# Kernel study: sketched linear attention, Fourier mix and MLP on one core — another form of the MLP, another handing-out of PSUM banks, wider q features, and the order of steps made for them

## The chip, the cores and the metric

One Trainium2 chip, one core of it. Times are device microseconds (us) of one execution, and the profile's span is about 1.8 us shorter than the time of the same run. A run is called slow when its time is more than 1.5% above the fastest run of the same kernel. The medians quoted are of all runs, the ratios of fast ones.

PE is the tensor engine, PEld its weight loads, DVE the vector engine, ACT the scalar engine, POOL the GpSimd engine. Memory outside the core is reached by DMA.

## The reference, cut to what matters

```
# per batch (4), head (4), 1088 rows, head size 32, sketch size 8
a, b   = S1 @ x, S2 @ x                      # 8 values each, for x = q and for x = k
phi(x) = outer(a, b)                         # 64 features
kv, z  = sum over rows of phi(k) x v, of phi(k)
out    = (phi(q) @ kv) / (phi(q) @ z + 1e-6)
# all heads side by side: x is (4, 1088, 128)
u  = x + real(fft over 128 of fft over 1088 of x)
un = (u - mean(u)) / sqrt(var(u) + 1e-6)     # per row
y  = u + relu(un @ w_ch1) @ w_ch2            # 128 -> 512 -> 128
```

## The kernel before

The kernel is one list of small steps for four batches, in attention (features of k and q, `kv`, numerator and denominator), Fourier mix and MLP. Every step has a name, and the text `ORDER` says in which order they are put down. The traces looked at here show the engines taking their own instructions in that order, so the text decides which work stands in an engine's queue.

```
ORDER = """
wm1 wm1 wm1 wm1 wm1 wm1 wt wm1 (...) kT0.0 pkr0 pab0.0 kT0.1
(... 7 lines cut ...)
qp2.3 q2.4 qa2.4 qp2.4 kT3.0 kv2.0 bb0.0 st0.0 kpr1 rs0.0 un0.0 kv2.1 kv2.2 bb0.1 st0.1 kc2 kt2 kz2
rs0.1 un0.1 tr0.0 nd2.0 ut0.0 rc2.0 mh0.0.0 re0.0.0 re0.0.1 mh0.0.1 re0.0.3 re0.0.2 nd2.1 rc2.1
(... 13 lines cut ...)
"""
for name in ORDER.split():
    step[name]()
```

Step names: `wm` warm-up matmul, `wt` sketch weights, `kT`, `qT` transposes, `pab`, `ka`, `kp` features of k (matmul, copy, product), `q`, `qa`, `qp` features of q, `kv`, `kc`, `kt`, `kz` the sums, `nd`, `rc` numerator and division, `fo` folding, `a`, `z`, `zr` the transform over rows. The MLP has eight groups of four tiles and two rests: `bb` u, `st` statistics, `rs` root, `un` normalized u, `tr` its transposition, `ut` copy (`ud` on DVE), `mh` hidden matmuls, `re` or `rd` relu, `mm` output matmuls, `ot` output copy.

PSUM in three pools of two buffers each; w has buffers of two banks:

```python
ps_w = ctx.enter_context(tc.tile_pool(name="ps_w", bufs=2, space=PSUM))   # pq, ph, pz: two banks each
ps_g = ctx.enter_context(tc.tile_pool(name="ps_g", bufs=2, space=PSUM))   # pab, pkr, pkv, pt, pnd, put
ps_u = ctx.enter_context(tc.tile_pool(name="ps_u", bufs=2, space=PSUM))   # pu
```

The MLP (cut): the group's u is normalized, transposed on PE, goes through the hidden layer, and the output is added to u in PSUM.

```python
def st(self):
    for i in range(self.nt):
        nc.vector.bn_stats(stats[:, :], self.pu[:, i, :])
        nc.vector.bn_aggr(self.mv[:, i, :], stats[:, :])
def rs(self):    # rstd = sqrt(var + eps), on ACT
def norm(self):  # un
    nc.vector.reciprocal(rstd[:, 0:nt], rstd[:, 0:nt])
    for i in range(nt):
        nc.vector.tensor_scalar(out=self.un[:, i, :], in0=self.pu[:, i, :],
                                scalar1=self.mv[:, i, 0:1], scalar2=rstd[:, i : i + 1],
                                op0=SUB, op1=MULT)
def tr(self):
    for i in range(self.nt):
        nc.tensor.transpose(self.put[:, 128 * i : 128 * i + 128], self.un[:, i, :], ident_b[:, :])
def ut(self, copy=nc.scalar.copy):
    copy(self.unT[:, 0:n], self.put[:, 0:n])
def m1(self, c2):                       # two hidden chunks into two banks
    for c in range(2):
        nc.tensor.matmul(ph[:, c, 0:n], w1_b[:, ...], self.unT[:, 0:n], start=True, stop=True)
def m2(self):
    for i in range(self.nt):
        for cc in range(4):
            nc.tensor.matmul(self.pu[:, i, :], self.ht[:, cc, ...], w2_b[:, cc, :], start=False, stop=(cc == 3))
```

The q features are made in four steps of 256 columns and one of 2 x 32 for each batch.

## Time and profile before

| | before |
|---|---|
| time, median of 3 runs | 140.47 us (139.18 to 143.3) |
| span of the profiled run | 138.7 us, granted clock 0.973 |
| PE busy, of the whole span | 108.0 us, 78% |
| PE busy in the middle, 9.34 to 110.3 us | 85.40 of 100.96 us |
| PE idle in the middle | 15.6 us |

The page of the kernel before: the span, the busy time of each engine (share of the span, instructions), and PE's busy tenths in 40 equal slices of the span.

```profile
span 138.7 us, 3380 instructions
...
PE 108.0 (78%) x1324; PEld 73.8 (53%) x1333; DVE 84.7 (61%) x249; ACT 62.2 (45%) x149; POOL 41.0 (30%) x86
...
PE   6795898899769979967789999299798677767520
```

No engine is full. The row of tenths shows where: PE is mostly at 7 to 9 tenths through the middle and falls to 6 to 7 in the last quarter. For the argument, the span is cut in three: a start up to the first feature matmul (in after up to the end of the warm-ups, 0.2 us past it), a middle up to the last matmul of the row transform, and a tail of MLP groups only. This is the view by stretches: length, busy us (instructions) of PE, PEld, DVE, ACT, POOL, then granted clock, DMA share and GB/s.

```profile
core 0: us, PE busy (x) PEld busy (x) DVE busy (x) ACT busy (x) POOL busy (x), PEclk, DMA share, GB/s
0.00:9.34 9.34, 7.34 (x21) 2.69 (x21) 4.18 (x16) 1.28 (x1) 8.43 (x31) 1.00 0.72 162
9.34:110.30 100.96, 85.40 (x1167) 62.40 (x1172) 65.44 (x176) 46.56 (x114) 31.33 (x54) 0.98 0.31 66
110.30:138.70 28.40, 15.26 (x140) 8.73 (x141) 15.11 (x58) 14.32 (x34) 1.29 (x2) 0.93 0.15 43
```

PE is busy 85% of the middle. Its 15.6 idle us (100.96 − 85.40) are the largest sum of idle time in the kernel. The view of PE's waits in the middle, longest in total first (us in total, times, longest):

```profile
engine line waited for: us in total, times, longest us
PE put L514 <- DVE un L507: 2.3, 1, 2.3
PE pab L280 <- DVE kp L290: 1.6, 1, 1.6
PE pnd L428 <- DVE xf L451: 1.4, 2, 1.1
PE pkv L397 <- DVE kpr_244 L290: 1.1, 1, 1.1
PE pnd L428 <- DVE kp L290: 1.1, 2, 0.7
```

Kinds of wait are listed there, of 0.2 to 2.3 us. What one looks like is seen in the timeline (start, length, engine, line, operation, and in brackets the idle time before it and who ended it):

```profile
61.81 0.41 PE L514 MATMUL put<-ident_b,un 128*128 128x128 bf16 x4
...
62.20 0.21 ACT L420 COPY kvz_94<-pt 64x66 f32<-64x66 f32 x1
...
63.58 0.30 ACT L499 ACTIVATE rstd<-mv,bias_eps 128x4 f32<-128x4 f32 x1 [1.17 <-DVE mv L494]
63.90 0.58 ACT L520 COPY unT<-put 128x512 bf16<-128x512 bf16 x1
...
64.54 1.02 PE L529 MATMUL ph<-unT,w_b 128*128 128x512 bf16 x3 [0.92 <-ACT unT L520]
```

The transposition (`put`) is over at 62.22 us. The copy that the hidden matmuls wait for starts only at 63.90, because it stands in ACT's queue behind the root of the *next* group (`rstd`), for which ACT sat idle for 1.17 us. PE then waits 0.92 us. The copy itself takes only 0.58 us.

Two groups of instructions that the change touches (busy us, mean ns, idle us before):

```profile
L374 DVE TENSOR_TENSOR qpT<-pq,qa 128x512 f32<-128x512 f32 x16 | 11.0, 687 | 14.1 <-ACT qa L368 14.0
...
L368 ACT COPY qa<-pq 128x512 f32<-128x512 f32 x16 | 9.2, 585 | 9.0 <-PE pq L357 8.9
```

And two lines of the timeline at the start, the first transposes of k and the first feature matmuls:

```profile
7.88 1.30 DVE L337 STREAM_TRANSPOSE kT<-kin_80 128x512 f32<-128x512 f32 x2 [1.89 <-DMA kin_80<-in_k_dram]
...
9.34 1.05 PE L280 MATMUL pab<-sblk,kT 128*128 128x128 f32 x8
```

### The profile page before, as it was taken

How to read it: one execution, taken by the hardware profiler on the slowest of the kernel's cores; microseconds unless marked ns; L12 is line 12 of the kernel's file. 1: busy time of each engine (PE TensorE's matmuls, PEld its weight loads, DVE VectorE, ACT ScalarE, POOL GpSimd, SP SyncE). 2: the span in 40 equal slices, each digit the busy share in tenths (PEclk: the TensorE clock that was granted, in tenths of full speed). 3: DMA queues.
4: the chain of work that ended last, by engine and by line, in shares of the span. 5: the costliest groups of instructions: out<-in, count | busy, mean ns of one | idle time of the engine just before them, and what ended most of it. 6: DMA issues, size and time to landing. Idle time of an engine off the chain costs nothing.

```text
span 138.7 us, 3380 instructions
## 1 busy us (share of the span) xinstructions
PE 108.0 (78%) x1324; PEld 73.8 (53%) x1333; DVE 84.7 (61%) x249; ACT 62.2 (45%) x149; POOL 41.0 (30%) x86
## 2 busy tenths in 40 slices
PE   6795898899769979967789999299798677767520
PEld 2254567587557635845777467078654434434310
DVE  5238828978489473698695326837661684584720
ACT  2101236189745653634664460244433068738320
POOL 7998980000930010700564130002443030000000
PEclk9999999999999999999999999959999999999995
DMA  3989979989800000000011200000202000220221
GB/s 113 237 134 216 210 157 222 174 165 254 139 4 7 0 0 0 5 0 5 0 43 37 72 3 5 0 0 2 61 19 74 2 19 5 66 69 19 76 59 38
DMA packets 27968, 9.40 MB, mean 68 GB/s; under 512 B 20400, under 2 KB 26928, under 8 KB 27952
## 3 DMA queue, kind: packets, MB, share of 16 engines
q1 hardware_dynamic: 26912, 8.66, 27.5%
q0 software_dynamic: 672, 0.26, 1.6%
q10 hardware_dynamic: 368, 0.27, 0.8%
q8 instruction: 10, 0.16, 0.5%
q14 instruction: 6, 0.05, 0.2%
HBM read 7.22 MB, written 2.23 MB: 68 GB/s over the span
## 4 chain that ended last, share of the span: by engine, by line
PE 45%; DVE 28%; POOL 9%; ACT 9%; issue 4%; another core or an unknown queue 0%; POOLq 0%; ACTq 0%; DVEq 0%
PE pq L357 11%; PE pnd L428 7%; DVE un L507 6%; PE pu L544 5%; PE pkv L397 5%; PE pz L572 5%; DVE stats L493 5%; DVE kp L290 4%; PE ph L529 4%; DVE mv L494 4%; POOL kq L177 3%; PE pz L574 2%; ACT qa L368 2%; DVE qT L342 2%; ACT ht L534 2%
## 5 line engine op out<-in xcount | busy, mean ns | idle before, releaser
L374 DVE TENSOR_TENSOR qpT<-pq,qa 128x512 f32<-128x512 f32 x16 | 11.0, 687 | 14.1 <-ACT qa L368 14.0
L534 ACT ACTIVATE ht<-ph 128x512 bf16<-128x512 f32 (+1 forms) x30 | 14.8, 565 | 6.1 <-PE ph L529 3.9
L368 ACT COPY qa<-pq 128x512 f32<-128x512 f32 (+1 forms) x20 | 10.1, 521 | 9.2 <-PE pq L357 9.1
L493 DVE BATCH_NORM_STATS2 stats<-pu 128x6 f32<-128x128 f32 x34 | 9.4, 276 | 7.0 <-PE pu L597 3.3
L544 PE MATMUL pu<-w_b,ht 128*128 128x128 bf16 x136 | 10.7, 220 | 3.5 <-ACT ht L534 2.4
L357 PE MATMUL pq<-qT,wa 32*64 32x256 f32 (+1 forms) x192 | 12.2, 338 | 0.5 <-DVE qpT L374 0.4
L529 PE MATMUL ph<-unT,w_b 128*128 128x512 bf16 (+1 forms) x34 | 9.0, 350 | 4.0 <-ACT unT L520 3.1
L507 DVE TENSOR_SCALAR un<-pu,mv,rstd 128x128 bf16<-128x128 f32 x34 | 11.8, 406 | 0.4
L357 PE MATMUL pq<-qT,wb 32*64 32x256 f32 (+1 forms) x192 | 11.4, 322 | 0.0
L290 DVE TENSOR_TENSOR kp<-ka,pab 128x1024 f32<-128x1024 f32 x8 | 9.7, 1207 | 2.9 <-ACT ka L286 2.9
L544 PEld LDWEIGHTS <-ht 128*128 128x128 bf16 x136 | 8.0, 98 | 6.0 <-ACT ht L534 3.8
L280 PE MATMUL pab<-sblk,kT 128*128 128x128 f32 x64 | 9.0, 284 | 2.3 <-DVE kp L290 1.6
L499 ACT ACTIVATE rstd<-mv,bias_eps 128x4 f32<-128x4 f32 (+1 forms) x10 | 3.0, 297 | 17.1 <-DVE mv L494 17.1
L280 PEld LDWEIGHTS pab<-sblk,kT 128*128 128x128 f32 x64 | 7.8, 191 | 3.4 <-DVE kp L290 1.8
L514 PE MATMUL put<-ident_b,un 128*128 128x128 bf16 x34 | 5.9, 225 | 4.8 <-DVE un L507 3.6
L286 ACT COPY ka<-pab 128x128 f32<-128x128 f32 (+1 forms) x10 | 2.5, 254 | 13.6 <-PE pab L280 13.6
L191 PE MATMUL warm<-wdummy 128*128 128x512 bf16 x18 | 7.2, 577 | 1.2 <-DVE wdummy L144 1.2
L445 DVE TENSOR_SCALAR rc<-pnd 128x8 f32<-128x8 f32 (+1 forms) x20 | 3.2, 160 | 7.8 <-PE pnd L428 4.9
L539 DVE TENSOR_SCALAR ht<-ph 128x512 bf16<-128x512 f32 (+1 forms) x10 | 4.5, 482 | 5.7 <-PE ph L529 3.9
L514 PEld LDWEIGHTS <-un 128*128 128x128 bf16 x34 | 2.9, 96 | 8.5 <-DVE un L507 8.0
L357 PEld LDWEIGHTS pq<-qT,wb 32*64 32x64 f32 x192 | 6.2, 132 | 2.0
L451 DVE TENSOR_TENSOR xf<-pnd,rc 128x256 f32<-128x256 f32 x16 | 6.8, 424 | 0.7
(245 smaller groups left out, 232.8 us busy)
## 6 DMA issues: line engine op xcount, KB each, us to landing
out_dram<-ot SPq DMA_DIRECT2D x32, 64.0 KB, 2.0
qin_76<-in_q_dram SPq DMA_DIRECT2D x1, 544.0 KB, 5.6
qin_77<-in_q_dram SPq DMA_DIRECT2D x1, 544.0 KB, 5.1
qin_78<-in_q_dram SPq DMA_DIRECT2D x1, 544.0 KB, 6.6
qin_79<-in_q_dram SPq DMA_DIRECT2D x1, 544.0 KB, 4.7
vin_84<-in_v_dram SPq DMA_DIRECT2D x4, 128.0 KB, 3.4
kin_81<-in_k_dram SPq DMA_DIRECT2D x4, 128.0 KB, 3.3
vin_85<-in_v_dram SPq DMA_DIRECT2D x4, 128.0 KB, 5.3
```

The lines of the kernel that those rows point to most:

```text
L280: nc.tensor.matmul(_v(self.ps, 0, 128, 32 * j, [[256, 2], [128, 2], [1, 32]]), lhsT, sblk2, start=True, stop=True, skip_group_check=True)
L290: nc.vector.tensor_tensor(out=_v(self.out, 0, 128, 0, [[64, n], [8, 8], [1, 8]]), in0=_v(self.ka, 0, 128, 0, [[8, n], [1, 8], [0, 8]]), in ...
L357: nc.tensor.matmul(pq[f0 : f0 + 64, g % 2, w, n * i : n * i + n], wt[32 * g : 32 * g + 32, :, :], self.qT[32 * g : 32 * g + 32, pr, c0 : c ...
L368: nc.scalar.copy(self.qa[c][:, :, 0:m], self.pq[c][:, :, 0, 0:m])
L374: nc.vector.tensor_tensor(out=qpT[:, prs[0], :, c0 : c0 + n], in0=pq[:, :, 1, 0:n], in1=qa[:, :, 0:n], op=MULT)
L428: nc.tensor.matmul(pnd[:, 2 * a + pr, :], self.qpT[:, pr, a, 32 + 128 * c : 160 + 128 * c], kvz[:, pr, :], start=True, stop=True, skip_gro ...
L493: nc.vector.bn_stats(stats[:, :], self.pu[:, i, :])
L507: nc.vector.tensor_scalar(out=self.un[:, i, :], in0=self.pu[:, i, :], scalar1=self.mv[:, i, 0:1], scalar2=rstd[:, i : i + 1], op0=SUB, op1 ...
L514: nc.tensor.transpose(self.put[:, 128 * i : 128 * i + 128], self.un[:, i, :], ident_b[:, :])
L529: nc.tensor.matmul(ph[:, c, 0:n], w1_b[:, 128 * cc : 128 * cc + 128], self.unT[:, 0:n], start=True, stop=True)
L534: nc.scalar.activation(out=self.ht[:, cc, 0:n], in_=self.ph[cc // 2][:, cc % 2, 0:n], func=ACT.Relu)
L544: nc.tensor.matmul(self.pu[:, i, :], self.ht[:, cc, 128 * i : 128 * i + 128], w2_b[:, cc, :], start=False, stop=(cc == 3), skip_group_chec ...
```

## The change

Its intent: to take the normalization out of the chain in front of the hidden layer, to let any step use any free PSUM bank, and to halve the number of q steps.

1. MLP. u is built twice, once as before and once transposed, straight from the transform, so that nothing has to be normalized before the first matmul. The weight is centred beforehand (which takes the mean out), and 1/std, being positive, passes through the relu and is applied to the output, with the sum, on DVE.
2. One PSUM tile of eight banks; a free bank is picked when a step is put down, always the one that has been free longest.
3. q features in 512 columns: two steps and a rest for each batch.
4. At the start, k of batch 0 is issued ahead of S on ACT's queue.
5. The text `ORDER` is made anew, all 23 lines of it (26 after).

```diff
 ORDER = """
-wm1 wm1 wm1 wm1 wm1 wm1 wt wm1 wm1 wm1 wm1 wm1 wm1 wm1 wm1 wm1 wm1 wm1 wm1 kT0.0 pkr0 pab0.0 kT0.1
-ka0.0 kp0.0 pab0.1 qT0 ka0.1 kp0.1 q0.0 qa0.0 kT1.0 qp0.0 ktr0 kv0.0 pbr0 kar0 q0.1 qa0.1 q0.2 kv0.1
+wm1 wm1 wm1 wm1 wt wm1 wm1 wm1 wm1 wm1 wm1 wm1 wm1 wm1 wm1 kT0.1 wq qT0.1 qT0.0 kT0.0 pab0.1 w1 wm1
+pkr0 wm1 wm1 wm1 pab0.0 ka0.1 ka0.0 ktr0 tf0 kT1.0 kT1.1 kp0.1 tfd kp0.0 qT1.0 qA0.1 qA0.0 qB0.0
 (... all other lines replaced too; cut ...)
+class Banks:
+    def __init__(self, n):
+        self.clock, self.at = n, list(range(n))
+    def take(self, n):
+        starts = [i for i in range(0, len(self.at), n)
+                  if all(a is not None for a in self.at[i : i + n])]
+        b0 = min(starts, key=lambda i: max(self.at[i : i + n]))
+        for i in range(b0, b0 + n):
+            self.at[i] = None
+        return b0
+    def drop(self, bn):
+        self.clock += 1
+        for i in range(bn[0], bn[0] + bn[1]):
+            self.at[i] = self.clock
-    ps_w, ps_g, ps_u = (three pools, as above)
+    pall = psum.tile([128, 8, 512], FP32, name="pall")
+    banks = Banks(8)
 (... start ...)
-    nc.scalar.dma_start(s12[...], S1), (s12[...], S2)      # first on ACT's queue
+        # after the four loads of k of batch 0, two of which are on ACT's queue:
+        nc.scalar.dma_start(s12[...], S1), (s12[...], S2)
 (... q features ...)
-    self.qa[c] = sb2.tile([128, 2, 256], FP32, name="qa", tag="qa")
+    self.qa[pr] = sb2.tile([128, 2, 512], FP32, name="qa", tag="qa")
 (... MLP ...)
+        def us(self, copy=nc.scalar.copy):      # u to SBUF, its bank comes free
+            copy(self.u_s[:, 0 : self.nt, :], self.pu[:, 0 : self.nt, :])
+            banks.drop(self.bnu)
-                nc.vector.bn_stats(stats[:, :], self.pu[:, i, :])
-                nc.vector.bn_aggr(self.mv[:, i, :], stats[:, :])
+                nc.vector.bn_stats(stats[:, i, :], self.u_s[:, i, :])
+            (four small operations for all tiles of the group give DM * var)
-        def tr(self):    # PE transposes of un
+        def tt(self):    # u transposed, from z, eight matmuls
-            nc.tensor.matmul(self.pu[:, i, :], self.ht[...], w2_b[:, cc, :], start=False, ...)
+            nc.tensor.matmul(self.pm[:, i, :], self.ht[...], w2_b[:, cc, :], start=(cc == 0 and i == 0), ...)
-            copy(ot[:, 0:nt, :], self.pu[:, 0:nt, :])
+            nc.vector.scalar_tensor_tensor(out=ot[:, i, :], in0=self.pm[:, i, :],
+                                           scalar=rstd[:, i : i + 1], in1=self.u_s[:, i, :], op0=MULT, op1=ADD)
```

## The prediction

> **What bounds it now.** No engine is full: the page shows PE 108.0 us (78% of 138.7), DVE 84.7, ACT 62.2. By stretches, PE is 88% busy from 14.4 to 58.2 us, 87% to 86.9, 78% to 108.5, but 67% from 108.5 to 133.7. Front and middle are nearly bound by PE; the last 25 us are latency. There the chain of waits repeats, per group of four tiles: stats and aggregate 1.7 us, rstd 0.3, reciprocal 0.2, un 1.37, transpose 0.23, copy 0.59, ph 0.5, four relus 2.04, pu matmuls 1.0, ot 0.58: about 8.5 us, one group each 5 us.
>
> **What changes, with costs.**
> 1. MLP. u is also built transposed, straight from z, so statistics, root and reciprocal leave the chain before the first matmul; 1/std (positive, so it passes through the relu) is applied at the end. Estimated chain: 0.9 (transposed u) + 0.6 copy + 0.6 + 2.0 relus + 0.3 (last matmuls, now chunk by chunk behind the relus) + 1.5 (scale-and-add, like un: 4 at 0.34, plus a reciprocal) = 5.9, about 2.7 shorter. Work hardly falls: transposes (0.23 streamed) become eight wider matmuls (0.67, estimate): PE +3.5 us in all. ACT trades ot copies for copies of u to SBUF. DVE: un becomes the final add; the aggregates become four small operations of about 0.2. Fewer DVE relus, -2.7; more DVE copies, about +2.7.
> 2. q in 512 columns: qa is 585 ns at 512 elements and 265 at 128, so 1012 at 1024 (estimate): ACT -1.3 us; qpT 687 at 512, about 1207 at 1024 (as kp shows): DVE -1.3. PE streams as many columns in half the matmuls (24, not 48, a batch): perhaps -1 us.
> 3. Banks by age: three pools of two buffers become one pool of eight banks. The Trainium skill ("PSUM — Partial Sum Buffer", Terms) gives eight 2 KiB banks and one matmul output of at most one bank, so 512 f32 columns fill one; the trace's 128x512 f32 outputs agree. This removes waits such as PE's for kp and xf (3.0 us listed for pab and pnd) and for ot (1.3).
> 4. Start. k of batch 0 is issued first; kT now waits 1.9 us for it and starts at 7.88: -1 us. v3 loads later. One f32 512-column matmul and a copy for the centred weight: about 1 us, hidden.
>
> **On the critical path.** Last stretch: four groups and a rest at about 4.2 instead of 5 us: -3.5 to -4. Middle: -3 (fewer hand-offs, more PE work). Start -1. Sum about -8 of 140.5: **132.0 us**, 8 in 10 between 127.5 and 137.0. Chances: faster by over 2% 0.88, within 2% 0.09, slower 0.03.
>
> **Right if the profile shows:** PE 107 to 112 us busy but 82% or more; no PE waits for un (now 3.6 us); the stretch after the last pz matmuls about 4 us shorter; qa near 1.01 and qpT near 1.21 us; kT about 1 us sooner; DVE down 1 to 6 us.
>
> **Wrong if:** statistics from SBUF or the scale-and-add cost much more than un (DVE, 64% busy in the last stretch, becomes the bound there); the SBUF copy of u, reused for the output, waits for stores; wider q steps starve PE while ACT takes 1 us; PE is really full in the middle, so its extra 3.5 us shows in full; or the clock is granted lower when PE is denser (it fell to 0.83 at 90 to 100 us).

## The result, and the profile after

The changed kernel takes 122.44 us (median of 4 runs, 121.13 to 125.66; the two fast ones took 121.13 and 121.66), the kernel before 141.08 beside it. The ratio of fast runs is 0.868, with a 95% interval of 0.849 to 0.887. Ratios are the mean time of one kernel's fast runs over that of the other's of the same rounds, so not quite the ratio of the medians quoted. The gain is about 19 us where 8.5 were predicted, and 122.4 lies outside the predicted 127.5 to 137.0.

The page of the kernel after:

```profile
span 119.8 us, 3138 instructions
...
PE 105.2 (88%) x1191; PEld 70.3 (59%) x1191; DVE 79.8 (67%) x247; ACT 62.4 (52%) x148; POOL 42.0 (35%) x86
...
PE   6069998999999999999999999999999998966710
```

PE's busy time has fallen by only 2.8 us, from 108.0 to 105.2, but its share of the span has risen from 78% to 88%, and its row is almost all nines from the fifth slice up to the tail. So most of the gain is idle time that vanished, not work. The two profiled runs had nearly the same granted clock (0.973 and 0.980) and their spans differ by 18.9 us, so the clock does not make the gain. The stretches (columns as before):

```profile
0.00:11.66 11.66, 6.53 (x16) 2.50 (x17) 5.14 (x19) 1.28 (x1) 10.57 (x34) 1.00 0.95 191
11.66:95.40 83.74, 83.14 (x1000) 56.94 (x1000) 58.85 (x159) 48.11 (x115) 30.22 (x51) 1.00 0.35 70
95.40:119.80 24.40, 15.50 (x180) 10.88 (x177) 15.86 (x69) 12.97 (x33) 1.23 (x2) 0.90 0.21 58
```

| stretch | before | after | difference | predicted |
|---|---|---|---|---|
| start | 9.34 | 11.66 | +2.3 | −1 |
| middle | 100.96 | 83.74 | −17.2 | −3 |
| of it PE busy | 85.40 | 83.14 | −2.3 | |
| of it PE idle | 15.6 | 0.6 | −15.0 | |
| tail | 28.40 | 24.40 | −4.0 | −3.5 to −4 |

The tail came as predicted. The start went the other way. The middle is nearly the whole surprise: the waits of PE there, which were of eighteen kinds, have all gone but two of the engine's own:

```profile
PE pall L458 <- issue: 0.4, 1, 0.4
PE pall L493 <- issue: 0.2, 1, 0.2
```

The two groups of the q features have doubled in width:

```profile
L418 DVE TENSOR_TENSOR qpT<-pall,qa 128x1024 f32<-128x1024 f32 x8 | 9.7, 1214 | 10.7 <-PE pall L405 9.7 <-ACT qa L413 1.0
...
L413 ACT COPY qa<-pall 128x1024 f32<-128x1024 f32 x8 | 8.1, 1016 | 3.8 <-PE pall L405 3.6
```

Both came as estimated (1.016 and 1.214 us, against 1.012 and 1.207). The Trainium skill ("VectorE: DVE Perf Modes", section on the TRN2 errata) gives cycle formulas with a fixed part, 172 plus the elements at 1.2 GHz for ScalarE from PSUM: an estimate from it is 570 ns at 512 elements and 997 at 1024. The trace agrees within 3% (585 and 1016). Fewer, longer copies pay the fixed part less often, and the busy time shows it: 9.2 us before, 8.1 after. What that is worth in time is asked below.

At the start, four lines of the timeline after:

```profile
7.02 0.26 PE L245 MATMUL pall<-ident_f,s_68 16*128 16x16 f32 x1 [3.95 <-DMA s_68<-in_S_dram]
...
7.21 4.45 PE L233 MATMUL pall<-wdummy 128*128 128x512 bf16 x10
...
7.71 0.71 DVE L393 STREAM_TRANSPOSE kT<-kin_74 128x512 f32<-128x512 f32 x1
...
11.45 1.06 PE L331 MATMUL pall<-sblk,kT 128*128 128x128 f32 x4
```

The sketch weights (L245) wait 3.95 us for S, whose load now stands behind k on ACT's queue; ten warm-up matmuls, which stand behind them in PE's queue, then hold PE until 11.66. The transposed k has been ready since 8.42 (7.71 + 0.71), and the first feature matmul starts at 11.45, 2.1 us later than before.

### The profile page after: what moved, and what is told of

Read it like the earlier page. It is cut to its first block, busy times and chain, and to the rows that moved or that the text cites. A ratio compares the mean times of both kernels' runs of the same rounds, so it can differ in the third digit from the quotient of the medians.

```text
span 119.8 us, 3138 instructions
## 1 busy us (share of the span) xinstructions
PE 105.2 (88%) x1191; PEld 70.3 (59%) x1191; DVE 79.8 (67%) x247; ACT 62.4 (52%) x148; POOL 42.0 (35%) x86
## 4 chain that ended last, share of the span: by engine, by line
PE 77%; DMA 7%; DVE 6%; ACT 3%; issue 2%; ACTq 1%; DVEq 0%
PE pall L405 13%; PE pall L493 13%; PE pall L458 8%; PE pall L331 8%; PE pall L658 7%; PE pall L614 5%; PE pall L233 4%; PE pall L595 4%; DMA s_68<-in_S_dram 4%; PE pall L660 3%; DMA out_dram<-us 3%; PE pall L680 3%; DVE stats L565 2%; DVE us L558 2%; PE pall L690 2%
## 5 line engine op out<-in xcount | busy, mean ns | idle before, releaser
L601 ACT ACTIVATE ht<-pall 128x512 bf16<-128x512 f32 (+1 forms) x36 | 18.2, 557 | 7.3 <-PE pall L595 7.2
L418 DVE TENSOR_TENSOR qpT<-pall,qa 128x1024 f32<-128x1024 f32 x8 | 9.7, 1214 | 10.7 <-PE pall L405 9.7
L614 PE MATMUL pall<-w_b,ht 128*128 128x128 bf16 x136 | 11.4, 220 | 2.0 <-ACT ht L601 0.9
L595 PE MATMUL pall<-uT,w_b 128*128 128x512 bf16 (+1 forms) x40 | 10.6, 347 | 1.8 <-ACT uT L587 1.0
L626 DVE SCALAR_TENSOR_TENSOR us<-pall,rstd,us 128x128 f32<-128x128 f32 x33 | 9.4, 345 | 1.8 <-PE pall L614 1.1
L413 ACT COPY qa<-pall 128x1024 f32<-128x1024 f32 x8 | 8.1, 1016 | 3.8 <-PE pall L405 3.6
L341 DVE TENSOR_TENSOR kp<-ka,pall 128x1024 f32<-128x1024 f32 x8 | 9.6, 1205 | 0.2 <-ACT ka L337 0.2
L331 PE MATMUL pall<-sblk,kT 128*128 128x128 f32 x64 | 9.4, 293 | 0.0
L331 PEld LDWEIGHTS pall<-sblk,kT 128*128 128x128 f32 x64 | 8.6, 206 | 0.8 <-issue 0.3
L405 PE MATMUL pall<-qT,wb 32*64 32x512 f32 x64 | 8.7, 610 | 0.0
L405 PE MATMUL pall<-qT,wa 32*64 32x512 f32 x64 | 8.4, 606 | 0.0
```

The source lines that it names most:

```text
L331: nc.tensor.matmul(_v(self.ps, 0, 128, 32 * j, [[256, 2], [128, 2], [1, 32]]), lhsT, sblk2, start=True, stop=True, skip_group_check=True)
L341: nc.vector.tensor_tensor(out=_v(self.out, 0, 128, 0, [[64, n], [8, 8], [1, 8]]), in0=_v(self.ka, 0, 128, 0, [[8, n], [1, 8], [0, 8]]), in ...
L405: nc.tensor.matmul(pq[f0 : f0 + 64, g % 2, :], wt[32 * g : 32 * g + 32, :, :], self.qT[32 * g : 32 * g + 32, pr, 32:544], start=True, stop ...
L418: nc.vector.tensor_tensor(out=self.qpT[:, pr, :, 32:544], in0=pq, in1=self.qa[pr][:], op=MULT)
L595: nc.tensor.matmul(ph[:, 0:n], w1_b[:, 128 * cc : 128 * cc + 128], self.uT[:, 0:n], start=True, stop=True)
L601: nc.scalar.activation(out=self.ht[:, cc, 0:n], in_=ph[:, 0:n], func=ACT.Relu)
```

## The experiments

All kernels gave correct results. Ratios are to the kernel before, in the same rounds on the same chip; its median was 142.2 to 142.5 us in all four sets.

| kernel | what it is | median us | ratio (95%) |
|---|---|---|---|
| b1_banks_only | before, with banks by age, old order | 139.87 | none (one fast run) |
| b2_old_order | all parts of the change, old order | 142.74 | 0.996 (0.984 to 1.009) |
| b4_new_mlp_only | before, with the new MLP, old order | 148.53 | 1.045 (1.031 to 1.058) |
| a3_old_mlp_in_after | after, with the old MLP | 160.35 | 1.124 (1.112 to 1.137) |
| c0_after_again | after | 121.52 | 0.857 (0.848 to 0.866) |
| a2_q_256 | after, with q in 256 columns | 121.43 | 0.857 (0.848 to 0.865) |
| a1_newest_bank | after, newest free bank first | 173.41 | 1.214 (1.196 to 1.231) |
| s1_early_start | after, with S loaded first | 119.83 | 0.844 (0.834 to 0.855) |
| r3_before_reordered | before, with another order only | 121.61 | 0.851 (0.843 to 0.858) |
| r4_banks_tuned | before, banks by age, order found for it | 115.53 | 0.817 (0.811 to 0.823) |
| r1_new_tuned | all parts, S first, order found for it | 116.07 | 0.814 (0.808 to 0.821) |
| r2_old_mlp_tuned | as r1, but the old MLP, order found for it | 113.30 | 0.793 (0.787 to 0.800) |

The theories: the gain is (M) the MLP's shorter chain, (B) the banks, (Q) the wide q steps, or (O) the new order, for which the others may or may not be needed.

### The parts in the old order: b1_banks_only, b2_old_order, b4_new_mlp_only

b1 takes the pools out of the kernel before and puts the eight banks by age in, everything else and the order as they were:

```diff
-            self.pu = ps_u.tile([128, 4, 128], FP32, name="pu", tag="u")
+            self.bnu, self.pu = ps(1, [[128, 4], [1, 128]])
 (... every PSUM tile so ...)
```

With it the transposition of un becomes a matmul with the identity, since the one PSUM tile is f32.

> The kernel before, its order of steps, its MLP and its 256-column q kept; only PSUM changes: one pool of eight banks, the oldest free bank handed out. Theory A (the three small pools made PE wait for DVE and ACT to free buffers): 131 to 136 us, PE idle in the middle at least halved from 15.6 us. Rival B (PE idled because of the order of the steps and the long chains, not for lack of banks): 138 to 141 us, PE idle in the middle 13 us or more.

Four runs: 136.74 (fast, clock 0.96) and 139.38, 140.37, 144.33 (slow, clock 0.92 to 0.87). With one fast run there is no ratio. The banks alone don't bring 19 us in the old order, but whether they bring 0 or 5 is not to be had from this run, and its profile is of a slow run (0.872), so its idle time is not used either. Inconclusive.

b2 is the other way round: every part of the change, the code of after line for line, but its order is the old one, translated to the new steps (the start is after's).

```diff
 ORDER (of after, behind the start)
-qT1.0 qA0.1 qA0.0 qB0.0 qa0.0 qp0.0 pbr0 kv0.0 qB0.1 ...
+qA0.0 qB0.0 qa0.0 qp0.0 kv0.0 pbr0 kar0 qA0.1 qB0.1 ...
```

> All code of the kernel after (new MLP, eight banks by age, q in 512 columns, its loads and start), but from the first k features on its steps stand in the order of the kernel before, translated step for step (one step held back for want of banks). Theory C (the re-made order of steps is most of the gain, the listed changes only allow it): 131 to 138 us with 8 us or more of PE idle in the middle. Rival D (the listed changes remove the waits by themselves, the order is a detail): 122 to 127 us.

142.74 us, ratio 0.996: nothing is gained, and the time is above even the range expected for the theory of the order; only the idle time came as that theory expected. The middle of its profiled run (a slow one, clock 0.922):

```profile
11.74:111.20 99.46, 89.02 (x1008) 62.93 (x1013) 61.11 (x167) 47.57 (x110) 29.64 (x51) 0.95 0.32 62
```

PE is idle for 10.4 us in it (99.46 − 89.02), where after has 0.6, and its longest waits there are for the division (2.4 us) and for k features (1.5). Over the whole span the longest are for copies of the transposed u and for relus, 4.5 us each, and most of these lie in the tail. All the parts that the title of the change names, put into the old order, are worth nothing in sum. They carry the late start with them, which costs about 2 us (s1 below).

b4 puts the new MLP alone into the kernel before, with its pools and its order (each MLP step translated):

```diff
-... bb0.0 st0.0 kpr1 rs0.0 un0.0 kv2.1 kv2.2 bb0.1 st0.1 kc2 kt2 kz2 rs0.1 un0.1 tr0.0 nd2.0 ut0.0 ...
+... bb0.0 us0.0 st0.0 kpr1 rs0.0 kv2.1 kv2.2 bb0.1 us0.1 st0.1 kc2 kt2 kz2 rs0.1 tt0.0 nd2.0 ut0.0 ...
```

> The kernel before with its pools, its q and its order, only the MLP changed to the unnormalized, directly transposed form. Theory E (the shorter MLP chain is what fills PE): 129 to 134 us. Rival F (in a fixed order with two-buffer pools the shorter chain frees nobody in the middle, only the last stretch gains): 135 to 139 us, the stretch after the last DFT matmuls 3 to 5 us shorter, the middle within 2 us.

148.53 us, 4.5% *slower*, which neither theory expected. Even the tail, where only MLP groups are left, is longer in its profiled fast run: 30.6 us (114.6 to 145.2), against 28.4, though at a lower granted clock there (0.81 against 0.93). A shorter chain on paper did not become a shorter one in the trace; PE's waits have only changed their names:

```profile
PE ph L546 <- ACT uT L537: 4.5, 4, 2.0
PE pm L563 <- ACT ht L552: 4.0, 4, 1.7
```

The wait for un became a wait for the copy of the transposed u, and most of both (3.1 and 3.5 us) lies in the tail: the copies and relus stand in ACT's queue where the old order put them. Theory M falls as a sufficient cause of the gain.

### The old MLP in the new order: a3_old_mlp_in_after

```diff
 (after, with st, rs, norm, tr, ut, m2, ot of before; un put ahead of tt; 21 steps held back so that
  no step waits for one behind it in the list)
```

> The kernel after (banks by age, 512-column q, its order) with the MLP of before put back: normalise, then transpose; u stays in its bank until the end. Root and normalisation stand just before the transposition; 21 steps had to be held back for want of banks, so the order is not tuned for it. Theory E (the MLP form is the main cause): 132 to 140 us, PE idle in the middle over 8 us. Rival G (banks and q carry it): 122 to 127 us.

160.35 us, 12% slower than before, with a granted clock of 0.847. PE's longest wait is for un:

```profile
PE pall L579 <- DVE un L572: 18.5, 10, 3.3
```

It is slower than either theory expected. By itself this looks like proof that the new MLP is the cause of the gain. It isn't: the order of after was made for the new MLP, with the transposed u close behind u, and the old chain does not fit it. r2 below shows the same code without that flaw.

### Parts taken out of after: c0_after_again, a2_q_256, a1_newest_bank, s1_early_start

c0 is after once more, on the chip of the next three.

> The kernel after unchanged, as the yardstick for the runs beside it: 121 to 124 us.

121.52 us, ratio 0.857.

a2 makes each q step in two halves of 256 columns, in the same place of the order:

```diff
-            nc.scalar.copy(self.qa[pr][:], pq)
+            for c0 in (0, 256):
+                nc.scalar.copy(self.qa[pr][:, :, c0 : c0 + 256], pq[:, :, c0 : c0 + 256])
 (... the matmuls and the products the same way ...)
```

> The kernel after and its order, but every q step cut into two halves of 256 columns (matmuls, copies and products; the rest part in 32 columns), as before. Theory (wide q is a small term: 8 x 0.16 us ACT, 8 x 0.15 us DVE, 4 x 0.45 us PE): 1 to 3 us slower than the kernel after. Rival (halves give finer hand-offs, so as fast or faster): within 0.5 us.

121.43 us, the same as c0: a miss for the expectation that it would be slower. The copies take 593 ns again instead of 1016, the products 677 instead of 1214, which is 0.5 us more on each of the two engines by their busy columns. PE is busy with q matmuls for 16.8 us in 256 columns, where it took 16.7 us in 512, and with the rests for 2.7 us in 32 columns, where it took 1.8 in 64 (overlaps counted once). None of this, not even the 0.9 us of PE, shows in the time. Theory Q is worth 0. The Trainium skill ("Perfetto Trace Analysis", on matmuls under Optimizing Tensor Performance) says that larger matmuls are more efficient; here that held between 32 and 64 columns, and between 256 and 512 it made no difference.

a1 changes one sign:

```diff
-        b0 = min(starts, key=lambda i: max(self.at[i : i + n]))
+        b0 = min(starts, key=lambda i: -max(self.at[i : i + n]))
```

> The kernel after and its order, but the bank freed last is handed out first instead of the one freed first. Theory (age is what keeps PE from waiting for the reader of a bank just released): 4 to 12 us slower, with new PE waits for ACT and DVE copies. Rival (with eight banks any free one does, the order alone counts): within 1.5 us.

173.41 us, 43% over c0, far more than expected. The line of busy times:

```profile
PE 121.2 (71%) x1184; PEld 77.1 (45%) x1191; DVE 81.0 (48%) x247; ACT 63.5 (37%) x148; POOL 41.9 (25%) x86
```

PE's share falls to 71%, with waits spread over many lines, the longest 3.4 us in total but for the wait for S. A bank is picked when the step is put down, and "free" then means that its last reader stands earlier in the list, not that this reader is done. The newest free bank is the one whose reader comes just before, so the matmul into it waits for that reader. With the oldest there are up to seven other banks' uses between. The same page and place of the Trainium skill say that matmul groups should rotate through the banks. Oldest first does that and newest first does the opposite, so the run agrees; the page gives no size, which is 52 us here.

s1 puts S first on ACT's queue, as before, takes three warm-ups out, and moves the first k, q and centring steps:

```diff
-wm1 wm1 wm1 wm1 wt wm1 wm1 wm1 wm1 wm1 wm1 wm1 wm1 wm1 wm1 kT0.1 wq qT0.1 qT0.0 kT0.0 pab0.1 w1 wm1
-pkr0 wm1 wm1 wm1 pab0.0 ka0.1 ka0.0 ...
+wm1 wm1 wm1 wm1 wm1 wm1 wt wm1 wm1 wm1 wm1 wm1 wm1 wm1 wm1 kT0.1 kT0.0 wq qT0.1 qT0.0 pab0.1 wm1
+pab0.0 ka0.1 ka0.0 ...
```

> The kernel after, but S1 and S2 are loaded first on their queue (as before), three warm-up matmuls fewer, and the first k features, q features and the centring of the weight put in the order in which their data land. Theory (the start lost 2.3 us against before because the first k features waited for S at 6.9 us and then for ten slow warm-up matmuls, and PE is full from there on, so the loss shows in full): 1.5 to 3 us faster than the kernel after. Rival (input DMA, 0.9 busy until 35 us, then holds PE instead): within 1 us.

119.83 us, 1.7 less than c0. The first transposes and the first feature matmuls in its timeline:

```profile
8.09 1.30 DVE L392 STREAM_TRANSPOSE kT<-kin 128x512 f32<-128x512 f32 x2 [3.38 <-DMA kin<-in_k_dram]
...
8.86 1.16 PE L330 MATMUL pall<-sblk,kT 128*128 128x128 f32 x8 [2.78 <-DVE kT L392]
```

The features start at 8.86 instead of 11.45 us (11.82 in c0). The start cost after about 2 us, and it was the prediction's "Start −1" that was wrong in sign.

### The order alone: r3_before_reordered

The order was what no run had changed alone. To find one that fits the *old* code, a small model was written: every engine takes its steps in the order of the list, each with its duration from the traces, and waits for its inputs and buffers; steps were moved about in it at random and what made the model shorter was kept. The model is an estimate: 142 us for the kernel before, 118 for the order that it found. r3 is the kernel before, line for line, with only the text exchanged.

```diff
 ORDER = """
-... kT3.0 kv2.0 bb0.0 st0.0 kpr1 rs0.0 un0.0 kv2.1 kv2.2 bb0.1 st0.1 kc2 kt2 kz2
-rs0.1 un0.1 tr0.0 nd2.0 ut0.0 rc2.0 mh0.0.0 re0.0.0 re0.0.1 mh0.0.1 re0.0.3 re0.0.2 nd2.1 rc2.1 ...
+... bb0.0 qa2.4 ktr1 qa2.1 pab3.0 qp2.1 ka3.1 kp3.1 fo1.1 qp2.4 q2.3 st0.0 ka3.0 kp3.0 pbr1 a1.0 rs0.0
+un0.0 qa2.3 pab2.1 kar1 bb0.1 kpr1 z1.0 ka2.1 tr0.0 qp2.3 a1.1 ud0.0 kp2.1 mh0.0.0 st0.1 z1.1 kv2.0 ...
 """
```

> The kernel before, line for line, with only the text of its order of steps exchanged for one found by my own search (a model of in-order engines, waits and buffers with the durations of the traces; it puts the old order at 142 us and this one at 118). Theory C (the order of the steps is the gain; the listed changes are not needed for it): 117 to 127 us, PE idle between the first k features and the last DFT matmuls under 8 us. Rival D (old MLP, small pools and narrow q cannot keep PE fed in any order): 132 us or more.

121.61 us, ratio 0.851 (0.843 to 0.858); after itself had 0.857 on another chip. **An order alone gives as much as the whole change, without one of the parts that the change names.** It is not the order of after, which does not suit the old MLP (a3). What b2 and r3 show together is that the parts in the old order gain nothing, and that a fitting order without the parts gains everything. The granted clock of r3's profiled run was 0.959, lower than the 0.973 of before, so it is not the clock either. The busy line and PE's row of its page, and its stretches:

```profile
PE 103.6 (87%) x1333; PEld 72.0 (60%) x1333; DVE 90.1 (75%) x258; ACT 56.6 (47%) x140; POOL 40.5 (34%) x86
...
PE   6949989999999999999999999999996695679420
```

```profile
0.00:8.68 8.68, 5.83 (x21) 2.12 (x22) 4.65 (x16) 1.28 (x1) 7.76 (x31) 1.00 0.69 160
8.68:95.90 87.22, 84.17 (x1191) 61.79 (x1191) 73.97 (x203) 46.08 (x118) 32.13 (x55) 1.00 0.38 79
95.90:119.70 23.80, 13.59 (x125) 8.09 (x124) 11.46 (x40) 9.20 (x21) 0.65 (x1) 0.79 0.17 48
```

PE is idle for 3.05 us in the middle (87.22 − 84.17), instead of 15.6, with the same instructions, the same three pools and the same old MLP. (The pages count 1324 and 1333 matmuls: nine records are missing from the trace of before, so a little of its idle time may be work that was not recorded.) The tail is 4.6 us shorter as well. The same place as in the timeline of before, the transposition of the first MLP group and what follows:

```profile
53.40 0.38 PE L514 MATMUL put<-ident_b,un 128*128 128x128 bf16 x4
...
53.62 0.63 PE L572 MATMUL pz<-stab,xp 128*128 128x273 bf16 x4
53.87 0.42 DVE L520 COPY unT<-put 128x512 bf16<-128x512 bf16 x1
...
54.41 0.64 PE L572 MATMUL pz<-stab,xm 128*128 128x273 bf16 x4
...
55.20 0.60 PE L529 MATMUL ph<-unT,w_b 128*128 128x512 bf16 x2
```

The copy of unT now stands on DVE, right behind one product, and is done at 54.29. PE meanwhile does the second half of the row transform of the *next* batch (`pz<-stab`, step `a1.1`, which the old order has at 79.67, some 18 us behind that place), and reaches the hidden matmuls (`ph`) at 55.20 without a wait. The Trainium skill ("Perfetto Trace Analysis", Optimization Strategy) says that where a kernel has regimes with different limits, interleaving them may help beyond work within each, and that one should look for the gaps on the busiest engine. The trace agrees with the second: 15.6 us of gaps became 3. That regimes with different limits were mixed is not shown.

Why this order and not the other has no clean test, but a count helps. From u to un, DVE and ACT need about 3.7 us (statistics 1.7, root 0.3, reciprocal 0.2, un 1.37, and the passing on). Adding up the durations of the PE work that the list puts between a group's u and its transposition gives, as an estimate over the eight groups, a median of 2.3 us in the old order, 4.1 in r3, and 6.0 in r4 below. The old order asks PE to come back before the result can be there.

### What the parts are worth in an order that fits: r4_banks_tuned, r1_new_tuned, r2_old_mlp_tuned

The same search was made for three other kernels. r4 is b1 (old MLP, q in 256 columns, old start, banks by age), with one hidden chunk in each step instead of two:

```diff
-            for c in range(2):
-                cc = 2 * c2 + c
-                bn, ph = self.ph[cc] = ps(1, [[1, 512]])
-                (matmul)
+            bn, ph = self.ph[cc] = ps(1, [[1, 512]])
+            (matmul)
 (and ORDER exchanged)
```

> The kernel before with its old MLP, its 256-column q and its start; only its PSUM pools become eight banks handed out by age (hidden-layer chunks in single banks), and the order is found by the same search for these steps. The model gives 112.8 us against 118.0 with the old pools (measured 121.6). Theory (in a fitting order the one pool is worth about 5 us, since it lets PE run ahead): 114 to 118 us. Rival (the order alone does it, the pool is a detail): 120 to 123 us.

115.53 us, ratio 0.817 (0.811 to 0.823), against 0.851 for r3: the pool of banks, together with an order found for it, is worth 5 to 6 us. How much of this is the pool alone is not shown, since the order and the steps of the hidden layer differ too. Its middle:

```profile
7.90:90.60 82.70, 80.88 (x1163) 59.53 (x1164) 67.79 (x189) 46.98 (x118) 33.75 (x58) 1.00 0.39 79
```

PE is idle for 1.8 us there, only 1.2 less than in r3; 3.3 us of the difference is busy time of PE (84.17 against 80.88), and no run says why. r1 has all parts of the change, S loaded first, and an order found for it. r2 is r1 with the old MLP (the diff is that of a3) and an order found for that.

```diff
 r1, to after:  S1 and S2 first on ACT's queue; ORDER exchanged
 r2, to r1:     st, rs, norm, tr, ut, m2, ot of before; ORDER exchanged
```

> All listed changes (new MLP, eight banks by age, 512-column q), the early start, and an order found by the same search. The model gives 115 us where it gives 123 for the early start in the kernel's own order (measured 119.8), so 111 to 116 us is expected if the model holds; 119 or more if its orders do not carry over to the chip.

> Eight banks by age, 512-column q, the early start of the run before, but the MLP of before (normalise, then transpose), in an order found by the same search for these steps. The model gives 112 us, for the directly transposed form 115, because the old form needs about 3.8 us less of PE. Theory H (in a fitting order PE is the limit, so the new MLP costs time instead of saving it): 1 to 4 us faster than the new MLP in its searched order. Theory E (the shorter MLP chain is worth something in any order): at least 2 us slower than it.

116.07 us (r1) and 113.30 us (r2). The old MLP is 2.8 us *faster* where each has its own order. The busy times, r1 first, then r2 (whose profiled run was a slow one, at clock 0.963, so its PE time is if anything too long):

```profile
PE 103.1 (90%) x1187; PEld 68.7 (60%) x1187; DVE 84.5 (74%) x256; ACT 58.7 (51%) x138; POOL 41.3 (36%) x86
```

```profile
PE 100.9 (89%) x1139; PEld 66.6 (59%) x1139; DVE 80.9 (71%) x241; ACT 61.8 (55%) x147; POOL 40.3 (36%) x86
```

PE is busy for 2.2 us more in r1, and it is the fullest engine (90% and 89%), so its extra work probably makes most of the 2.8 us; a2 warns that extra PE time need not show. In these two orders the change's trade, a shorter chain for wider matmuls, is a loss. r2, at 113.3 us and 20.7% below the kernel before, is the fastest kernel.

## Why the prediction was wrong

**The tail, "−3.5 to −4": right in size, but not for the reason given.** It shortened by 4.0 us. The reason given was the shorter chain. b4, with the new MLP in the old order, has a tail 2.2 us *longer* (30.6 us, with a granted clock of 0.81 there against 0.93 before), and r3, with the old MLP in another order, one 4.6 us shorter. So the tail, too, can be shortened by where its steps stand; the new MLP is neither enough for it nor needed. That the number came as predicted is in part luck. In their searched orders the tail is 18.8 us in r1 and 21.6 in r2, with 11.1 and 13.2 us of PE work in it, so what the new MLP brings to a tail in a fitting order is not settled.

**"Middle: −3 (fewer hand-offs, more PE work)": wrong, and the step that failed.** The term measured −17.2 us. The prediction had read "Front and middle are nearly bound by PE" from a PE that was 78 to 88% busy in three stretches, and took that as a limit. Of the 101 us, 15.6 were idle, and 15.0 of these went. The prediction then counted the gain from the waits that the *named* parts remove (3.0 us for kp and xf, 1.3 for ot), and overlooked that the diff's first part exchanges the order of all steps. r3 shows an order alone to be worth 20.8 us of 142.4 (142.4 − 121.6), and b2 shows the named parts in the old order to be worth nothing. What the order removes is not one wait but eighteen small ones.

**"PE +3.5 us in all": off in sign for the whole, right in kind.** PE busy fell by 2.8 us. The extra matmuls of the new MLP are there (r1 against r2: +2.2 us). What the prediction missed is that PE's busy time also depends on the order: r3, with the matmuls of before, has 103.6 us instead of 108.0. Of these 4.4 us, 1.7 are in the warm-ups (7.2 and 5.5 us for 18 matmuls); the cause of the rest stays open. It is not the mean granted clock, which was lower in r3 (0.959 against 0.973). Over all runs the clock tends to be higher where PE is busier: 0.98 to 0.99 in fast runs of after (PE 88% of the span), 0.93 to 0.97 in those of before (78%). The Trainium skill ("TensorE: Matmul & The Clock Gate", Part 1) says that activity releases the throttle; the direction agrees here, but not everywhere: a1, with PE at 71%, was granted 0.92, and a3, with 77%, only 0.85.

**"Banks by age … removes waits": not settled.** Waits of 4.3 us in all were named. 5 to 6 us were found for the banks and an order fitted to them (r3 to r4), nothing clear in the old order (b1), and the rule by which a bank is picked carries 52 us in after's order (a1).

**q in 512 columns: right in the profile, worth nothing in time.** qa took 1.016 and qpT 1.214 us, as estimated. "Perhaps −1 us" of PE came too: the q matmuls keep PE busy for 19.5 us before and 18.6 after, nearly all of the difference in the rests, which went from 32 to 64 columns. a2 takes both back (19.5 us) and its time is the same.

**"Start −1": wrong in sign, +2.3.** The prediction moved k forward and did not ask what k's place was taken from: S, which the warm-ups stand behind. kT did start sooner, but by 0.2 us, not 1. s1 gets 1.7 us of it back.

**The signs in the profile.** No PE wait for un: seen, but after has no un to wait for. PE share of 82% or more: seen, 88%. PE 107 to 112 us busy: 105.2, just outside. DVE down 1 to 6 us: seen, 4.9. The tail 4 us shorter: seen. Of the dangers named, stores did hold up a reuse of u's copy once, for 1.2 us of DVE. A lower clock for a denser PE did not come: after's middle, where PE is busy for 83.14 of 83.74 us, shows 1.00.

**What stays open.** The searched orders come from a model and a random search, so the 2.8 us between r1 and r2 hold for those two orders. r4 also splits the steps of the hidden layer, and r3 and r4 ran on different chips. Which property of an order does it (the distance between u and its transposition, or the mixing of batches) was counted, not tested. b1 is inconclusive.

## What to carry to other kernels

An engine that is 85% busy with its idle time in many small waits is not bound: before costing the named parts of a change, ask what a better order of the same instructions would do, and read the whole diff for a changed order. For every result that leaves an in-order engine and comes back, count the work that stands in between and compare it with the round trip; where there is less, move independent work (of another batch) into the gap. Judge a part only in an order made for it: the same old MLP was 12% slower than the kernel before in one order (a3) and 21% faster in another (r2, where S is also loaded first).

## What the Trainium skill lacked or had wrong

- "Perfetto Trace Analysis" (matmuls, under Optimizing Tensor Performance) says to rotate through PSUM banks, but neither what this is worth nor what "free" means when all is laid out ahead: oldest first 121.5 us, newest first 173.4.
- The same page (Optimization Strategy) mentions interleaving regimes as something that may help. It tells how to look for gaps, but not how to size the gain, nor that the order of the steps in an engine's queue can be the whole of it: 142.4 to 121.6 us here, with no instruction changed.
- The same page's "Larger matmuls are more efficient" names no width at which this ends: 256 against 512 columns made no difference to PE (16.8 and 16.7 us busy), 32 against 64 did (2.7 and 1.8), and neither showed in the time (121.43 and 121.52).
- "VectorE: DVE Perf Modes" (section on the TRN2 errata): its formulas give, as an estimate, 194 ns for 128 elements from SBUF and 258 from PSUM. The statistics on 128 elements took 280 ns from SBUF and 276 from PSUM, so the single instruction did not get shorter in SBUF. The section itself says that its formula from SBUF is too low and gives a fixed term of about 150 cycles instead, an estimate of 290 ns, which fits; for PSUM it has no such remark. (The busy time of all 34 fell from 9.4 to 7.5 us, because four in a row overlap: 0.87 us a group.)
